# Part of a w2 block loaded ahead of wo in 125 and 3 rows, and three filler products on TensorE

## The chip, the cores and the metric

The kernel runs on one core of one Trainium2 chip. The metric is the device time of one execution in microseconds; lower is better. A core has the engines TensorE (PE in the profile, PEld for its loads of weights), VectorE (DVE), ScalarE (ACT), GpSimd (POOL) and SyncE (SP), and sixteen DMA engines that carry the loads which SP issues.

## The reference

A decode step for two sequences with one new token each. Attention of 32 query heads over 8 key and value heads in a window of the last 4096 positions, and beside it a dense layer with the Mish activation; a sigmoid gate mixes the two.

```
x: (2, 1, 512)   W = 4096, Dh = 128, F = 1792
q = (x @ wq) as (2, 32, 1, 128)
k, v = the last W positions of k_cache, v_cache, each of 8 heads used by 4 query heads
a = softmax(q k^T * Dh^-0.5) v, as (2, 1, 4096), @ wo          # wo: 4096 x 512
h = x @ w1 + b1;  b = (h * tanh(softplus(h))) @ w2             # w1: 512 x 1792, w2: 1792 x 512
g = sigmoid(sum(x * gate_w))
out = g * a + (1 - g) * b
```

All data are f32.

## The kernel before

Everything that is large is loaded once, by SP, into three buffers of 128 x 16384 f32 that are used in turn (`stream`): `wq`, then one tile for each of the eight key and value heads (`kv0` to `kv7`), then `w12`, then `wo`. Before the launch the arrays are laid out so that a load is 128 rows, one for each partition, each of them contiguous.

For each head, TensorE multiplies the queries with the keys (`scores`, L148), VectorE takes the maximum (L151), ScalarE the exponential (L153), TensorE turns the result (`turned`, L160) and multiplies it with the values (`values`, L172). The load of the next head into a buffer is issued when the products of the head that had the buffer are done. In all of these products the array is split into four strips of 32 columns, one product in each, so four run side by side. An f32 product appears as two passes in the profile.

The tile `w12` holds w1 (7168 columns), the first four heads' rows of wo (2048 columns) and w2. w2 has 14 blocks of 128 rows, 512 columns each; the first seven come with w1 in one load. The tile `wo` holds the other 28 heads' rows, in two loads, of 20 and of 8 heads (`WO`, L291). The other seven blocks of w2 come last, in three loads of 4, 2 and 1 blocks (`CUTS`, L294), into the rest of the tile `w12`. So SP's queue at the end is: kv7, w12, wo (20 heads), wo (8 heads), w2 (4 blocks), w2 (2), w2 (1). The tile `wo` needs the buffer of kv6, so SP waits for that head's products between the issue of w12 and that of wo.

What TensorE does at the end, in this order: `hidden` (x with w1), `outputs` (the normalized heads), then `project` (L305) with the four heads of wo that lie in `w12`, `middle` with the seven blocks of w2 that came with w1, the 28 heads in `wo`; all of these add into `acc`. Then `output(1)` (`finish`, L315) with the first four of the late blocks of w2, into `fin`; `finish(fold2, asum)`, which adds a copy of `acc` into `fin`; `output(2)` and `output(3)` with the last blocks. VectorE copies `fin` to `res` (L348) and SP stores it (L349). `pin` keeps the order of the products as written. Ahead of the store, SP waits until the last eight loads have landed (L343).

Of the kernel before, what the change touches and what calls it, by code (L numbers as in the profile page):

```python
# [8 lines left out]
F32 = mybir.dt.float32  # L9
# [4 lines left out]
P = 128  # L14
B = 2
D = 512
# [8 lines left out]
NJ = 4  # L25
# [6 lines left out]
FC = F // P  # L32
# [7 lines left out]
CUTS = (0, 7, 11, 13, 14)  # L40
WO = (1, 6, 8)
ROWS = (24, 104)
WIDE = 2 * Q - B
AHEAD = DC * F + WO[0] * REP * D


@with_exitstack
def decode_kernel(ctx: ExitStack, tc: tile.TileContext, res, stored, small, wqh, wqt, kv_in, w12, wo, w2, out):
    nc = tc.nc
# [5 lines left out]
    ps_s = ctx.enter_context(tc.tile_pool(name="ps_s", bufs=2, space=bass.MemoryType.PSUM))  # L55
    ps_1 = ctx.enter_context(tc.tile_pool(name="ps_1", bufs=1, space=bass.MemoryType.PSUM))

    loads = []

    def load(name, *parts):  # L60
        t = stream.tile([P, 2 * CHUNK], F32, tag="s", name=name)
        x = 0
        for cols, src in parts:
            loads.append(nc.sync.dma_start(t[:, x : x + cols], src))  # L64
            x += cols
        return t
# [20 lines left out]
    ones = const.tile([P, P], F32, name="ones")  # L87
# [54 lines left out]
    pin = tc.keep_in_program_order  # L142

    def scores(kv, t):
        sc = ps_s.tile([P, 512], F32, tag="sc", name=f"sc{kv}")
        for m in range(BN):
            for j in range(NJ):
                nc.tensor.matmul(sc[Q * j : Q * j + Q, :], qz[:, kv, m * Q : m * Q + Q],  # L148
                                 t[:, (m * NJ + j) * 512 : (m * NJ + j + 1) * 512],
                                 start=(m == 0), stop=(m == BN - 1))  # L150
        nc.vector.tensor_reduce(mx[:, kv : kv + 1], sc, axis=AX.X, op=ALU.max, negate=True)  # L151
        p = work.tile([P, 512], F32, tag="p", name=f"p{kv}")
        nc.scalar.activation(p, sc, AF.Exp, bias=mx[:, kv : kv + 1], accum_out=ls[:, kv : kv + 1])  # L153
        return p
# [11 lines left out]
    def values(kv, pT, t, c0=0, c1=NT):  # L166
        if kv % 2 == 0 and c0 == 0:
            pair[0] = ps_1.tile([P, 2, BN * DH], F32, tag="o", name=f"o{kv}")
        o = pair[0][:, kv % 2, :]
        for c in range(c0, c1):  # L170
            for j in range(NJ):
                pin(nc.tensor.matmul(o[Q * j : Q * j + Q], pT[:, c, Q * j : Q * j + Q],  # L172
                                     t[:, (c * NJ + j) * 512 : (c * NJ + j + 1) * 512],
                                     start=(c == 0), stop=(c == NT - 1)))
        if kv % 2 and c1 == NT:
            wide = [P, 2 * BN, DH]
            om = single.tile(wide, F32, tag="om", name=f"om{kv}")
            ov = om.rearrange("p (k m) d -> p k m d", m=BN)
            nc.vector.tensor_tensor(  # L179
                ov, pair[0].rearrange("p k (m d) -> p k m d", m=BN),  # L180
                pick[:, None, :, None].to_broadcast([P, 2, BN, DH]), op=ALU.mult)
            nc.vector.tensor_reduce(od[:, kv - 1 : kv + 1], ov.rearrange("p k m d -> p k d m"),  # L182
                                    axis=AX.X, op=ALU.add)
# [89 lines left out]
    for kv in range(HKV):  # L273
        t = load(f"kv{kv}", (2 * CHUNK, kv_in[kv]))
        p = scores(kv, t[:, :CHUNK])
# [7 lines left out]
            r = shares(kl)  # L283
        values(kv, pT, t[:, CHUNK:], 2, NT)
    w12_t = load("w12", (AHEAD + CUTS[1] * D, w12))

    def flat(src, cuts, size):
        for f0, f1 in zip(cuts, cuts[1:]):
            yield (f1 - f0) * size, src[f0 * size * P : f1 * size * P].rearrange("(p x) -> p x", p=P)

    wo_t = load("wo", *flat(wo, [f - WO[0] for f in WO], REP * D))  # L291
    x = AHEAD + CUTS[1] * D
    for cols, src in flat(w2, [f - CUTS[1] for f in CUTS[1:]], D):
        loads.append(nc.sync.dma_start(w12_t[:, x : x + cols], src))  # L294
        x += cols
    hidden(w12_t)
# [6 lines left out]
    def project(j, lhsT, rhs, n):  # L303
        n_col[j] += 1
        return nc.tensor.matmul(acc[Q * j : Q * j + Q, :], lhsT, rhs,  # L305
                                start=(n_col[j] == 1), stop=(n_col[j] == n))
# [5 lines left out]
    def finish(lhsT, rhs):  # L312
        for j in range(NJ):
            y = j % 2 * (Q - B)
            nc.tensor.matmul(fin[Q * j : Q * j + Q, :], lhsT[:, y : y + Q], rhs[:, j * P : (j + 1) * P],  # L315
                             start=(done[0] == 0), stop=(done[0] == n_fin - 1))
        done[0] += 1

    def middle(f0, f1):
        for f in range(f0, f1):  # L320
            x = AHEAD + f * D
            pin(project(f % NJ, actT[:, f, :], w12_t[:, x : x + D], n_of[f % NJ]))

    first = WO[0] * REP
    for x in range(HQ):
        w = w12_t[:, DC * F + x * D :] if x < first else wo_t[:, (x - first) * D :]
        if x == first:
            middle(0, CUTS[1])
        pin(project(x % REP, oT[:, x, :], w[:, :D], n_of[x % REP]))
    asum = work.tile([P, D], F32, tag="p", name="asum")  # L330
    nc.scalar.copy(asum, acc)

    def output(i):
        for f in range(CUTS[i], CUTS[i + 1]):
            x = AHEAD + f * D
            finish(act2[:, f - CUTS[1], :], w12_t[:, x : x + D])
# [72 lines left out]
```

## Time and profile before

| | |
|---|---|
| median of three runs | 219.33 us (219.32 to 219.41) |
| profiled execution, span from the first to the last instruction | 217.6 us |
| TensorE busy | 113.0 us (52%) |
| DMA, rate over the span | 419 GB/s |
| chain that ended last | DMA 77%, PE 18% |
| mean granted TensorE clock | 0.867 |

For the profiled execution the profile gives the span and no other time; 1.7 us of the median lie around it. In the profile, a line such as `206.00 7.91 PE acc L305 x56` of a chain or a timeline gives the start and the length in us, the engine, the tile written, the line of the kernel and the number of instructions. In a table of windows each row gives a stretch, its length, the busy time and number of instructions of PE, PEld, DVE, ACT and POOL, then the clock granted to TensorE (1.00 is full speed), the share of the sixteen DMA engines at work, and GB/s. The queue q1 carries the loads and the store, q8 the engines' own instructions.

### The profile page before, as it was taken

The page shows a single profiled execution, that of the slowest core. Times are in us where ns is not written, and L with a number is a line of the kernel's source. Part 1 is how long each engine was busy: PE and PEld are TensorE (multiplying, and loading weights), DVE is VectorE, ACT ScalarE, POOL GpSimd, SP SyncE. Part 2 cuts the span into 40 slices and gives each one's busy share as a digit, 9 for nine tenths or more (in the row PEclk, how much of TensorE's full clock was granted, in tenths as well). Part 3 has the DMA queues.
Part 4 walks back from the last instruction along what each step waited for, and adds up shares of the span by engine and source line. Part 5 has one row for each costly group of instructions (what it writes and reads, how often), then busy time and mean ns, then how long its engine had stood idle before and what let it go on. Part 6 is the DMA issues. An engine that isn't in the chain of part 4 may idle for free.

```text
span 217.6 us, 1836 instructions
## 1 busy us (share of the span) xinstructions
PE 113.0 (52%) x822; PEld 33.8 (16%) x822; DVE 21.5 (10%) x32; ACT 15.5 (7%) x34; POOL 8.0 (4%) x30
## 2 busy tenths in 40 slices
PE   0000798477046608543660754286075418758596
PEld 0000322112011102101110210012011001214123
DVE  0000000010001230100123010010501001251000
ACT  2000001111001100200110020002002000301001
POOL 8000000000000000000000000000000000102100
PEclk9999999979658985995998599769759967999979
DMA  9797988898899889989998999899989999989892
GB/s 361 337 506 337 581 385 385 385 569 385 385 398 566 385 376 446 518 385 398 446 497 385 410 434 506 385 422 422 497 385 434 410 432 452 452 364 482 375 404 113
DMA packets 2550, 91.38 MB, mean 420 GB/s; under 512 B 416, under 2 KB 496, under 8 KB 752
## 3 DMA queue, kind: packets, MB, share of 16 engines
q1 hardware_dynamic: 2544, 91.28, 97.3%
q8 instruction: 6, 0.10, 0.2%
HBM read 91.24 MB, written 0.04 MB: 419 GB/s over the span
## 4 chain that ended last, share of the span: by engine, by line
DMA 77%; PE 18%; ACT 2%; DVE 1%; SPq 1%; issue 0%; ACTq 0%
DMA kv<-in_kv 61%; DMA wo<-in_wo 16%; PE sc L148 7%; PE o L172 5%; PE acc L305 4%; ACT p L153 1%; DVE mx L151 1%; PE pp L160 1%; PE fin L315 1%; ACT pT L161 1%; SPq L64 0%; SPq L70 0%; DVE res L348 0%; ACTq L161 0%; ACTq L153 0%
## 5 line engine op out<-in xcount | busy, mean ns | idle before, releaser
L148 PE MATMUL sc<-kv,qz 128*32 128x512 f32 x256 | 44.1, 851 | 54.1 <-DMA kv<-in_kv 54.1
L172 PE MATMUL o<-kv,pT 128*32 128x512 f32 x256 | 29.5, 596 | 5.8 <-ACT pT L161 5.8
L128 PE MATMUL qp<-wq,x 128*32 128x512 f32 x64 | 12.1, 799 | 23.0 <-POOL x L92 23.0
L148 PEld LDWEIGHTS sc<-kv,qz 128*32 128x32 f32 x256 | 9.9, 150 | 87.6 <-DMA kv<-in_kv 60.7
L151 DVE TENSOR_REDUCE mx<-sc 128x1 f32<-128x512 f32 x8 | 5.5, 691 | 112.4 <-PE sc L148 112.4
L153 ACT ACTIVATE p<-sc,mx 128x512 f32<-128x512 f32 x8 | 5.5, 687 | 131.2 <-DVE mx L151 131.2
L160 PE MATMUL pp<-ident,p 128*128 128x128 f32 x32 | 5.3, 287 | 12.1 <-ACT p L153 12.1
L172 PEld LDWEIGHTS o<-kv,pT 128*32 128x32 f32 x256 | 7.3, 109 | 20.9 <-issue 13.1
L305 PE MATMUL acc<-wo,padded 128*32 128x512 f32 x56 | 7.9, 728 | 2.2 <-DMA wo<-in_wo 2.2
L182 DVE TENSOR_REDUCE od<-om 128x256 f32<-128x1024 f32 x4 | 7.6, 1900 | 0.1
L128 PEld LDWEIGHTS qp<-wq,x 128*32 128x32 f32 x64 | 2.5, 137 | 28.9 <-POOL x L92 23.0
L179 DVE TENSOR_TENSOR om<-o,pick 128x1024 f32<-128x1024 f32 x4 | 4.9, 1225 | 19.3 <-PE o L172 19.3
L196 POOL TENSOR_TENSOR ms<-ms,top 8x64 f32<-8x64 f32 x2 | 0.6, 309 | 159.0 <-DVE top L194 159.0
L160 PEld LDWEIGHTS pp<-ident,p 128*128 128x128 f32 x32 | 3.4, 140 | 18.6 <-ACT p L153 18.6
L161 ACT COPY pT<-pp 128x512 f32<-128x512 f32 x8 | 4.7, 585 | 6.2 <-PE pp L160 6.2
L235 PE MATMUL hp<-w,x 128*32 128x512 f32 (+1 forms) x32 | 3.6, 543 | 2.3 <-DMA w<-in_w 2.3
L305 PEld LDWEIGHTS acc<-wo,padded 128*32 128x32 f32 x56 | 2.1, 129 | 8.0 <-issue 4.9
L305 PE MATMUL acc<-w,padded 128*32 128x512 f32 x22 | 2.8, 601 | 0.4 <-DVE padded L226 0.4
L117 DVE RECIPROCAL g<-g 128x2 f32<-128x2 f32 x1 | 0.2, 166 | 22.4 <-POOL g L116 22.4
L134 PE MATMUL qt<-ident,qs 128*128 128x128 f32 x8 | 1.3, 287 | 1.4 <-ACT qs L131 1.4
L112 PEld LDWEIGHTS zp<-xg,ones 128*128 128x128 f32 x8 | 1.8, 327 | 1.7 <-issue 1.7
L131 ACT ACTIVATE qs<-qp 128x512 f32<-128x512 f32 x2 | 1.2, 597 | 10.6 <-PE qp L128 10.6
(65 smaller groups left out, 31.3 us busy)
## 6 DMA issues: line engine op xcount, KB each, us to landing
wq<-in_wqt SPq DMA_DIRECT2D x1, 7168.0 KB, 21.4
w<-in_w SPq DMA_DIRECT2D x1, 6400.0 KB, 41.1
wo<-in_wo SPq DMA_DIRECT2D x1, 5120.0 KB, 34.8
wo<-in_wo SPq DMA_DIRECT2D x1, 2048.0 KB, 39.3
wq<-in_wqh SPq DMA_DIRECT2D x1, 1024.0 KB, 4.9
w<-in_w SPq DMA_DIRECT2D x1, 1024.0 KB, 41.3
w<-in_w SPq DMA_DIRECT2D x1, 512.0 KB, 42.0
w<-in_w SPq DMA_DIRECT2D x1, 256.0 KB, 42.1
```

The source lines that it names most:

```text
L128: nc.tensor.matmul(qp[Q * k : Q * k + Q, :], x32[:, c, :], w[:, c, k, :], start=(c == 0), stop=(c == DC - 1))
L148: nc.tensor.matmul(sc[Q * j : Q * j + Q, :], qz[:, kv, m * Q : m * Q + Q], t[:, (m * NJ + j) * 512 : (m * NJ + j + 1) * 512], start=(m == ...
L151: nc.vector.tensor_reduce(mx[:, kv : kv + 1], sc, axis=AX.X, op=ALU.max, negate=True)
L153: nc.scalar.activation(p, sc, AF.Exp, bias=mx[:, kv : kv + 1], accum_out=ls[:, kv : kv + 1])
L160: pin(nc.tensor.transpose(pp[:, c, :], p[:, c * P : (c + 1) * P], ident))
L161: nc.scalar.copy(pT, pp)
L172: pin(nc.tensor.matmul(o[Q * j : Q * j + Q], pT[:, c, Q * j : Q * j + Q], t[:, (c * NJ + j) * 512 : (c * NJ + j + 1) * 512], start=(c == 0 ...
L179: nc.vector.tensor_tensor(ov, pair[0].rearrange("p k (m d) -> p k m d", m=BN), pick[:, None, :, None].to_broadcast([P, 2, BN, DH]), op=ALU ...
L182: nc.vector.tensor_reduce(od[:, kv - 1 : kv + 1], ov.rearrange("p k m d -> p k d m"), axis=AX.X, op=ALU.add)
L235: nc.tensor.matmul(hp[Q * j : Q * j + Q, :n], x32[:, c, :], w[:, c, j * FG * P : j * FG * P + n], start=(c == 0), stop=(c == DC - 1))
L305: return nc.tensor.matmul(acc[Q * j : Q * j + Q, :], lhsT, rhs, start=(n_col[j] == 1), stop=(n_col[j] == n))
L315: nc.tensor.matmul(fin[Q * j : Q * j + Q, :], lhsT[:, y : y + Q], rhs[:, j * P : (j + 1) * P], start=(done[0] == 0), stop=(done[0] == n_fi ...
```

## The change

Of the first late block of w2, 384 of its 512 columns (`LOW`) are taken out of the load of four blocks and are loaded right behind w12, ahead of wo, by two loads: partitions 0 to 124 (`MOST` = 125 rows) and partitions 125 to 127 (3 rows), of 1536 bytes a row. The load of four blocks shrinks from 2048 to 1664 columns; the host lays w2 out accordingly. The tile, its columns and what is computed from them stay the same. On TensorE, three products of the constant `ones` (128 x 128) with the first 3 x 512 columns of w1 stand between `middle` and the first product with the tile `wo`; they write the tile `idle` in PSUM, which nothing reads.

```diff
+MOST = 125
+LOW = (NJ - 1) * P
...
     w12_t = load("w12", (AHEAD + CUTS[1] * D, w12))
+    at = AHEAD + CUTS[1] * D
+    for p0, p1 in ((0, MOST), (MOST, P)):
+        loads.append(nc.sync.dma_start(
+            w12_t[p0:p1, at : at + LOW], w2[p0 * LOW : p1 * LOW].rearrange("(p x) -> p x", p=p1 - p0)))
...
     wo_t = load("wo", *flat(wo, [f - WO[0] for f in WO], REP * D))
-    x = AHEAD + CUTS[1] * D
-    for cols, src in flat(w2, [f - CUTS[1] for f in CUTS[1:]], D):
+    x = at + LOW
+    ends = [0] + [(f - CUTS[1]) * D - LOW for f in CUTS[2:]]
+    for cols, src in flat(w2[P * LOW :], ends, 1):
         loads.append(nc.sync.dma_start(w12_t[:, x : x + cols], src))
         x += cols
...
         if x == first:
             middle(0, CUTS[1])
+            idle = ps_s.tile([P, 512], F32, tag="sc", name="idle")
+            for k in range(3):
+                pin(nc.tensor.matmul(idle, ones, w12_t[:, k * 512 : (k + 1) * 512], start=True, stop=True))
...
-    w2 = np.concatenate([w2[f:t].transpose(1, 0, 2).ravel() for f, t in zip(CUTS[1:], CUTS[2:])])
+    w2 = w2[CUTS[1] :].transpose(1, 0, 2).reshape(P, (FC - CUTS[1]) * D)
+    ends = [0, LOW] + [(f - CUTS[1]) * D for f in CUTS[2:]]
+    w2 = np.concatenate([w2[:, x0:x1].ravel() for x0, x1 in zip(ends, ends[1:])])
```

## The prediction

> **What bounds the kernel now.** I read the page first (span, engines, queues, chain), then the chain in order of time, then the timeline of the last 17 us.
>
> ```profile
> span 217.6 us, 1836 instructions
> PE 113.0 (52%) x822; PEld 33.8 (16%) x822; DVE 21.5 (10%) x32; ACT 15.5 (7%) x34; POOL 8.0 (4%) x30
> q1 hardware_dynamic: 2544, 91.28, 97.3%
> q8 instruction: 6, 0.10, 0.2%
> HBM read 91.24 MB, written 0.04 MB: 419 GB/s over the span
> DMA 77%; PE 18%; ACT 2%; DVE 1%; SPq 1%; issue 0%; ACTq 0%
> ```
>
> The loads fill 97.3% of the sixteen DMA engines' time. No byte is added or taken away by this change, so up to about 200 us nothing can move; all of it is decided in the tail, where the chain leaves the DMA engines and runs on TensorE:
>
> ```profile
> 171.11 34.85 DMA wo<-in_wo
> 205.96 0.04 issue
> 206.00 7.91 PE acc L305 x56
> 213.91 1.83 PE fin L315 x64
> 215.74 0.02 issue
> 215.77 0.29 DVE res L348
> ```
>
> The first wo load lands at 205.96, 56 passes of wo's products take 7.91 us, 64 passes of the last stage 1.83 us, then the copy and the store. But DMA is not far behind. The queue's issues and the time from issue to landing:
>
> ```profile
> 171.97 1.43 SPq L294 DMA_DIRECT2D w<-in_w  x3
> w<-in_w SPq DMA_DIRECT2D x1, 1024.0 KB, 41.3
> w<-in_w SPq DMA_DIRECT2D x1, 512.0 KB, 42.0
> w<-in_w SPq DMA_DIRECT2D x1, 256.0 KB, 42.1
> ```
>
> Three issues in 1.43 us start at about 171.97, 172.45 and 172.95, so w2's three blocks land at 213.3, 214.5 and 215.1. What must still follow the last landing is the last block's eight passes:
>
> ```profile
> 213.73 1.06 PE L315 MATMUL fin<-w,padded 128*32 128x128 f32 x32
> 214.62 0.42 PE L315 MATMUL fin<-asum,padded 128*32 128x128 f32 x8
> 214.86 0.84 PE L315 MATMUL fin<-w,padded 128*32 128x128 f32 x24
> ```
>
> Eight passes more cost 1.06 - 0.84 = 0.22 us, so the last eight of the 24 alone take 0.84 - 0.44 = 0.40 us. After the landing at 215.1 and 0.04 us of issue that is an end at 215.55 by DMA alone, against 215.74 by TensorE. **Two chains end within 0.2 us of each other**; whoever shortens only one gets 0.2 us at most.
>
> Both have a visible fault. TensorE's is the clock:
>
> ```profile
> 203.14:206.55 3.41, 1.23 (x14) 0.25 (x12) 0.00 (x0) 0.00 (x0) 0.00 (x0) 1.00 0.86 368
> 206.55:209.96 3.41, 3.41 (x24) 0.89 (x20) 0.00 (x0) 0.00 (x0) 0.00 (x0) 0.50 1.00 425
> 201.01 2.81 PE L305 MATMUL acc<-w,padded 128*32 128x512 f32 x22 [0.43 <-DVE padded L226]
> ```
>
> In the windows, the third number from the right is the granted clock. After a stretch with 1.23 us of work in 3.41 it was 0.50 for the next 3.41 us: while wo's first products ran. The DMA engines' fault is that they do not finish together:
>
> ```profile
> 212.80:213.00 0.20, 0.20 (x8) 0.13 (x4) 0.00 (x0) 0.00 (x0) 0.00 (x0) 1.00 0.99 389
> 213.20:213.40 0.20, 0.20 (x8) 0.02 (x1) 0.00 (x0) 0.00 (x0) 0.00 (x0) 1.00 0.49 195
> 213.60:213.80 0.20, 0.20 (x8) 0.07 (x4) 0.00 (x0) 0.00 (x0) 0.00 (x0) 1.00 0.40 164
> 214.00:214.10 0.10, 0.10 (x16) 0.10 (x8) 0.00 (x0) 0.10 (x1) 0.00 (x0) 1.00 0.33 123
> 214.40:214.60 0.20, 0.20 (x16) 0.12 (x6) 0.00 (x0) 0.17 (x1) 0.00 (x0) 1.00 0.26 102
> 214.70:214.80 0.10, 0.10 (x12) 0.10 (x12) 0.00 (x0) 0.00 (x0) 0.00 (x0) 1.00 0.01 0
> ```
>
> The last two numbers are the share of the sixteen engines at work and GB/s. Until 213.0 all work; by 213.6 six are left (0.40 x 16), by 214.4 four, and at 214.7 none. Ten are done at 213.0 to 213.5, six run about 1.3 us longer. Six is also the number of packets on the instruction queue above. I read it so: each fetch of instructions went in between the loads of another engine and set it back by 1.3 us (none is set back twice: the tail would be 2.6 us long).
>
> **The change part by part.** *Removed from the tail:* w2's first block loses 384 columns, 128 x 1536 bytes, on each engine eight rows of 1536 bytes = 12,288 bytes. At full share the window above moved 425 GB/s, 26.6 per engine: 0.46 us less behind wo, on all sixteen.
>
> *Added ahead of wo:* the same 196,608 bytes as loads of 125 and 3 rows. Every load of the trace has 128 rows (the store 80), so how 125 are shared no row shows. I take equal shares: 125 = 5 x 25, five engines get 25 rows each, 38,400 bytes; of the other three rows one each goes to three of these. The nearest price for rows this short is the 2 KB rows of the last block, 102 GB/s at a share of 0.26: 24.5 GB/s per engine, 1.57 us; by the 26.6 of long rows it is 1.44. I take 1.55. The five engines are then 1.55 us later at wo, and 1.55 - 0.46 = 1.1 us later at the end. The bounds from both sides: shared evenly over sixteen, 0.46 us each, nothing at the end; all on one engine, 7.4 us.
>
> [...]
>
> *SP's queue* gets two more issues, at 0.33 to 0.48 us each. They stand behind w12's issue, where SP then waits for wo's buffer until 171.11, so they delay nothing:
>
> ```profile
> 152.92 0.33 SPq L64 DMA_DIRECT2D w<-in_w  x1
> 171.11 0.82 SPq L64 DMA_DIRECT2D wo<-in_wo  x2
> SPq L343 <- DMA w<-in_w: 4.2, 3, 2.4
> SPq L349 <- DVE res L348: 0.9, 1, 0.9
> ```
>
> The wait ahead of the store (L343) covers the last eight loads as before, and SP then still waited 0.9 us for the copy; it binds at no point.
>
> *Three products of the constant with w1:* each is a matmul over the whole array and 512 columns, two passes as every f32 product here. Four passes of 32 columns that run side by side come every 0.43 us, from the values' products:
>
> ```profile
> 50.37 3.69 PE o L172 x32
> ```
>
> (32 passes in 3.69 us less the 0.6 us of the last one give about 0.43 per four.) A pass over all columns takes as long as the four: 6 x 0.43 = 2.6 us. They start when the last pass of w2's first products has streamed, about 203.7, and end at 206.2 to 206.4. The stretch from 203.14 to 206.55 is then filled, so I expect the clock to stay at 1.00. Who waits behind them on TensorE are wo's products; wo's load lands at 205.96 on the late engines, and on five clean ones at 205.96 - 1.3 + 1.55 = 206.2. So they cost 0 to 0.4 us in their place, and 56 passes then take 13 x 0.43 + 0.6 = 6.2 us instead of 7.91: done at 212.6 instead of 213.9. They write a PSUM buffer whose last reader, head 7's exponential, was done long before.
>
> *The sum, if the five engines are clean ones.* Late engines: last data at 214.7 - 0.46 = 214.25. The five: 213.0 to 213.5 plus 1.1 = 214.1 to 214.6. Last data therefore between 214.25 and 214.6, and the landing, 0.4 us behind the data as now (214.7 to 215.1), at 214.65 to 215.0; I take 214.8. TensorE by then: first block of w2 at 213.3 - 0.46 = 212.85, or 213.0 on the five; 1.06 us of passes to 214.1, the sum's eight passes inside that wait, second block at 214.05 to 214.2. TensorE waits for the last block, so DMA sets the end: 214.8 + 0.04 + 0.40 = 215.24 instead of 215.74, **0.50 us less**. Copy and store are unchanged. The profiled span is 217.6 and the median 219.33, so 1.7 us lie around the span; I leave them as they are: 219.33 - 0.50 = **218.83 us**, with 218.65 to 219.0 by the bounds.
>
> **The rivals.** *A late engine among the five (slower).* No view numbers the engines. If one of the six that a fetch set back also takes 25 rows, it ends 1.1 us after 214.7: landing at 216.2, end at 216.64, 0.9 us more, 220.2. If it is one of the two that were done by 214.2, landing 215.7, 0.45 us more, 219.8. It decides as soon as a single late engine is among the five, because an engine may take 0.46 us over its present load and no more. [...]
>
> *The 128 rows are shared evenly after all.* Then it is only a reordering; the last landing stays at 215.1 and the end at 215.55: 219.14.
>
> *The half-speed stretch is not in the timed executions.* It hangs on where a 3.41 us stretch falls on the wait of 2.2 us before wo. If the timed runs had none, they ended by DMA at 215.55 already, and clean engines give 0.31 us less: 219.02. [...]
>
> *The clock drops nevertheless, or the three products take longer:* wo's products from 206.3 at 7.91 us, then 1.83: end at 216.05, 0.3 us more, 219.64.
>
> *All 125 rows on one engine:* 7.4 - 0.46 - 1.3 us after the present last data: about 225.
>
> **How the numbers follow.** Clean engines 0.60 (of it 0.10 with no slow stretch before), a late one among the five 0.25, even shares 0.08, clock or products 0.05, one engine 0.02. A measurement of this kernel tells about 0.2%, 0.44 us, from no change. Faster by more than that is most of the clean case with the slow stretch: 0.44. Within 0.2%: the rest of the clean case, even shares, and a little of the others: 0.29. Slower: 0.27. The likeliest case alone spans 218.65 to 219.0; the range is 218.6 to 219.9, which takes in even shares, the clock, and the milder half of the late engine, and leaves out 220.2 and 225.
>
> **What would show it.** Right: granted clock 1.00 from 206.5 to 210; some 6.2 us for wo's 56 passes; a share of the DMA engines that falls to zero within about 0.4 us in place of 1.7; the chain's last DMA step is w, not wo, and ends at 214.8. Wrong: a share of 0.06 to 0.3 that lasts past 214.7 (a late engine got more), or an unchanged staircase (even shares); a clock of 0.50 after 206.5; a seventh packet on the instruction queue, 1.3 us more on one engine.

## The result and the profile after

The changed kernel takes 220.60 us in the median against 219.32; the ratio is 1.0055, with an interval of 1.0039 to 1.0071. It is slower by half a per cent, and it scatters: eleven runs lie between 219.49 and 223.91 us, where those of the kernel before lie between 219.15 and 220.06. The profiled execution is the slowest of them, 223.91 us; the ratios here and below leave out executions over 1.5% above the fastest of their kernel (here 223.91 and 223.54), so a reading of this profile counts only where the profile of another kernel below shows the same.

The page of the changed kernel, against 217.6 us and 113.0 us of TensorE before:

```profile
span 222.0 us, 1850 instructions
PE 123.4 (56%) x828; PEld 38.0 (17%) x828; DVE 21.4 (10%) x32; ACT 15.5 (7%) x34; POOL 8.0 (4%) x30
q8 instruction: 6, 0.10, 0.2%
DMA 59%; PE 24%; another core or an unknown queue 10%; ACT 3%; DVE 2%; issue 1%; SPq 1%; POOL 0%; ACTq 0%; DVEq 0%; POOLq 0%
```

Six passes were added, yet TensorE is busy 10 us longer. The end of its chain of waits (start, length, what):

```profile
203.66 5.34 PE acc L312 x22
209.00 2.98 PE idle L338 x6
...
212.33 5.92 PE acc L312 x53
...
219.04 1.12 PE fin L322 x32
220.19 0.29 DVE res L358
```

The last wait for a DMA is gone from the tail. From w12's landing on TensorE waits for no DMA and is late: the 22 first products with wo and w2 take 5.34 us (before: 2.81), the fillers follow on the path, and wo's products begin at 212. wo's first load had landed at 206.8, 32.8 us after its issue at 174.01:

```profile
174.01 0.84 SPq L66 DMA_DIRECT2D wo<-in_wo  x2
```

```profile
wo<-in_wo SPq DMA_DIRECT2D x1, 5120.0 KB, 32.8
```

Why it is late, its timeline and its table of windows say (clock, share of the DMA engines and GB/s are the last three numbers):

```profile
194.77 5.33 PE L237 MATMUL hp<-w,x 128*32 128x512 f32 x32 [3.29 <-DMA w<-in_w]
```

```profile
195.72:199.14 3.42, 3.42 (x23) 0.88 (x19) 0.00 (x0) 0.00 (x0) 0.00 (x0) 0.50 1.05 455
...
202.55:205.96 3.41, 2.98 (x16) 1.18 (x19) 0.46 (x2) 0.00 (x0) 1.16 (x5) 0.50 0.91 394
205.96:209.38 3.42, 3.42 (x15) 0.84 (x8) 0.00 (x0) 0.00 (x0) 0.00 (x0) 0.50 1.02 438
```

The half clock, which stood under wo's products before, now stands under x with w1 and under the first products, ahead of the fillers. The DMA side, from the same view:

```profile
186.00:204.00 18.00, 13.05 (x94) 5.30 (x96) 5.07 (x10) 1.76 (x5) 2.33 (x9) 0.86 1.00 411
```

```profile
214.00:214.20 0.20, 0.20 (x8) 0.08 (x1) 0.00 (x0) 0.00 (x0) 0.00 (x0) 1.00 0.67 266
...
214.40:214.60 0.20, 0.20 (x8) 0.07 (x4) 0.00 (x0) 0.00 (x0) 0.00 (x0) 1.00 0.61 236
...
214.80:215.00 0.20, 0.20 (x8) 0.07 (x4) 0.00 (x0) 0.00 (x0) 0.00 (x0) 1.00 0.32 123
215.00:215.20 0.20, 0.20 (x8) 0.13 (x4) 0.00 (x0) 0.00 (x0) 0.00 (x0) 1.00 0.01 0
```

The bytes moved as planned: from 214.0 to 214.6 nine to eleven of the sixteen engines work (0.58 to 0.67), not six. The trace has every packet with its start, its length and its bytes. If each is joined to the one that starts where it ends, five engines carry nearly all rows of 1536 bytes, and none of the five is one of the six late engines (ends at 214.6 to 214.7, and at 215.0 to 215.1): five and six make the eleven. But the end is 215.0 and not 214.25 to 214.6; it was 214.7 before. The engines to which nothing was added are done by 213.3 to 213.8, where before they were done at 213.0 to 213.5, although each had 0.46 us less to carry.

Two suspects remain: the fillers, and the loads.

### The profile page after: what moved, and what is told of

The parts are those of the page before. It is cut to its first block, busy times and chain, and to the rows that moved or that the text cites. A ratio compares the mean times of both kernels' runs of the same rounds, so it can differ in the third digit from the quotient of the medians.

```text
span 222.0 us, 1850 instructions
## 1 busy us (share of the span) xinstructions
PE 123.4 (56%) x828; PEld 38.0 (17%) x828; DVE 21.4 (10%) x32; ACT 15.5 (7%) x34; POOL 8.0 (4%) x30
## 4 chain that ended last, share of the span: by engine, by line
DMA 59%; PE 24%; another core or an unknown queue 10%; ACT 3%; DVE 2%; issue 1%; SPq 1%; POOL 0%; ACTq 0%; DVEq 0%; POOLq 0%
DMA kv<-in_kv 59%; PE sc L150 10%; PE acc L312 5%; PE o L174 5%; ACT p L155 1%; PE idle L338 1%; DVE mx L153 1%; PE fin L322 1%; PE pp L162 1%; PE ol L226 1%; ACT pT L163 1%; SPq L66 0%; PE ht L252 0%; POOL ms L198 0%
## 5 line engine op out<-in xcount | busy, mean ns | idle before, releaser
L150 PE MATMUL sc<-kv,qz 128*32 128x512 f32 x256 | 45.9, 882 | 49.3 <-DMA kv<-in_kv 49.3
L174 PE MATMUL o<-kv,pT 128*32 128x512 f32 x256 | 32.5, 647 | 5.8 <-ACT pT L163 5.8
L237 PE MATMUL hp<-w,x 128*32 128x512 f32 (+1 forms) x32 | 5.3, 749 | 3.3 <-DMA w<-in_w 3.3
L312 PE MATMUL acc<-wo,padded 128*32 128x512 f32 x56 | 6.4, 593 | 0.0
L312 PE MATMUL acc<-w,padded 128*32 128x512 f32 x22 | 5.3, 1061 | 0.4 <-DVE padded L228 0.4
L312 PEld LDWEIGHTS acc<-wo,padded 128*32 128x32 f32 x56 | 3.1, 110 | 2.4
L338 PE MATMUL idle<-w,ones 128*128 128x512 f32 x6 | 3.0, 644 | 0.0
L237 PEld LDWEIGHTS hp<-w,x 128*32 128x32 f32 x32 | 1.4, 137 | 7.2 <-DMA w<-in_w 4.2
L322 PE MATMUL fin<-w,padded 128*32 128x128 f32 x56 | 2.3, 274 | 0.0
## 6 DMA issues: line engine op xcount, KB each, us to landing
wo<-in_wo SPq DMA_DIRECT2D x1, 5120.0 KB, 32.8
```

Source lines behind the costliest of these rows:

```text
L237: nc.tensor.matmul(hp[Q * j : Q * j + Q, :n], x32[:, c, :], w[:, c, j * FG * P : j * FG * P + n], start=(c == 0), stop=(c == DC - 1))
L338: pin(nc.tensor.matmul(idle, ones, w12_t[:, k * 512 : (k + 1) * 512], start=True, stop=True))
```

## The experiments

Theory A: the fillers use up the time in which TensorE waited for wo, so that half clock ahead of them reaches the end. Theory B: the loads cause the loss, by a later w12 and wo. Later, theory C: the loads cost by the way their rows are dealt to the engines.

**The loads without the fillers** (changed kernel):

```diff
-            idle = ps_s.tile([P, 512], F32, tag="sc", name="idle")
-            for k in range(3):
-                pin(nc.tensor.matmul(idle, ones, w12_t[:, k * 512 : (k + 1) * 512], start=True, stop=True))
```

> The loads of 125 and 3 rows without the three filler products. Theory A (the fillers use up the time in which TensorE used to wait for wo, so that a stretch at half clock ahead of them now reaches the end; the loads cost little): 219.4 to 219.7 us, with a spread under 0.5 us, since the last landing of the changed kernel, 215.4, and 0.44 us after it end 0.1 to 0.2 us later than before. Theory B (the loads cause it: they stretch the other engines' packets, w12 lands 0.7 us later, and TensorE's chain starts later): 220.4 to 220.6 us with the spread of the changed kernel.

Measured: 220.08 us (219.48 to 221.03), ratio 1.0028 [1.0016, 1.0041]. This is between the two expectations, so the loads carry a part of the loss. The chain of this kernel:

```profile
170.92 35.66 DMA wo<-in_wo
...
206.62 7.78 PE acc L312 x56
214.40 1.84 PE fin L322 x58
```

wo lands 0.62 us later than before (206.58 for 205.96), and the products behind it run at half clock as they did before (7.78 and 7.91 us). Its windows:

```profile
206.41:209.82 3.41, 3.20 (x16) 0.80 (x20) 0.00 (x0) 0.00 (x0) 0.00 (x0) 0.50 1.02 437
```

```profile
186.00:204.00 18.00, 13.48 (x116) 5.29 (x117) 5.22 (x11) 1.76 (x5) 2.85 (x11) 1.00 0.99 411
```

From 186 to 204 us the engines were as busy as before (0.99) but moved 411 GB/s and not 426: the kernel before has this row:

```profile
186.00:204.00 18.00, 13.81 (x113) 5.34 (x113) 5.42 (x11) 1.76 (x5) 2.85 (x11) 1.00 0.99 426
```

15 GB/s over 18 us are 0.27 MB, 0.63 us of the whole rate. The transfers take longer; nobody waits. The packets say which ones. The rows of 1536 bytes are under way from 191.6 to 193.9 us, mostly five at a time. wo's first load has 128 rows of 40,960 bytes: before, one took 2.00 us, from 192.95 on, right behind an instruction packet (192.02, 0.94 us), and all others 1.51; here 22 take 1.63 to 2.28 us, and all 22 start between 191.5 and 194.1.

**The fillers without the loads** (kernel before, with the three lines above added):

> The three filler products without the new loads. Theory A: median 219.8 to 220.5 us, spread over 1 us, the slow executions with half clock in the stretch of x with w1 or of the first products with wo and w2. Theory B: 219.0 to 219.3 us, at most 0.2 us faster than before, since w12 lands when it did before.

Measured: 219.56 us (219.17 to 221.62), ratio 1.0014 [0.9993, 1.0036]: the scatter of theory A, but a median between the two expected ranges and a shift that is not clear of none. The profiled execution, 219.94 us, is one of the upper half; its chain:

```profile
200.96 4.47 PE acc L305 x22
205.43 2.77 PE idle L331 x6
208.20 6.15 PE acc L305 x56
214.35 1.83 PE fin L315 x64
```

The first products run at half clock (granted 0.50 from 201.8 to 205.2 us; 4.47 us for 2.81), so the fillers end at 208.2 instead of 206.4, 2.3 us behind wo's landing at 205.9 in this execution. In exchange wo's products take 6.15 us, as forecast.

**One load of 128 rows at the same place, no fillers** (the kernel of the loads alone):

```diff
-    for p0, p1 in ((0, MOST), (MOST, P)):
+    for p0, p1 in ((0, P),):
```

> The same 384 columns at the same place in one load of 128 rows, no fillers. If the loads cost by their shape (rows on five engines that cross the other engines' transfers): w12 lands 41.1 us after its issue as before, not 42.1, and the time is 219.2 to 219.4 us. If they cost by their place ahead of wo: as the loads of 125 and 3 rows, w12 at 42 us.

Measured: 219.52 us, ratio 1.0007 [0.9998, 1.0016]. Its windows:

```profile
186.00:204.00 18.00, 13.97 (x108) 5.61 (x110) 5.46 (x11) 2.46 (x8) 2.85 (x11) 0.92 1.00 428
```

The same bytes stand at the same place, and the rate stays at 428 GB/s; each of the 128 rows of wo's first load takes 1.51 us. So the shape costs, not the place. The time is a little above the expected range, and w12 landed 42.3 us after its issue, the sign that was named for the other case. But the issue came 1 us earlier than before (151.90 for 152.92), and the landing is at 194.2 for 194.0: here the time from the issue is no measure of the loads.

**Fillers ahead of x with w1 too** (the kernel with the fillers alone):

```diff
+    early = ps_s.tile([P, 512], F32, tag="sc", name="early")
+    for k in range(3):
+        pin(nc.tensor.matmul(early, ones, t[:, k * 512 : (k + 1) * 512], start=True, stop=True))
     hidden(w12_t)
```

> Three filler products with the last head's tile ahead of x with w1, and the three ahead of wo's products; no new loads. Theory A: the clock is full from the last head on, the fillers ahead of wo end by 206.4, and DMA sets the end: 219.0 to 219.3 us with a spread under 0.5 us. If it is the fillers' own 2.6 us that cost, and not the clock ahead of them: 220 us or more, slower than with the second three alone.

Measured: 219.48 us, ratio 1.0005 [0.9993, 1.0017], but from 219.11 to 223.83. The median is nearer theory A's range than the rival's, but the narrow spread is missing: seven of ten runs lie below 219.7, the others at 220.33, 222.51 and 223.83. So more fillers do not make the clock safe. The profiled execution, 219.46 us, has no half clock in the tail; what the runs at 220.33 and above have, no profile shows.

**112 and 16 rows** (the loads alone):

```diff
-MOST = 125
+MOST = 112
```

> [...] Theory C (what costs is that engines write to partitions that another engine is writing): between 219.7 and 220.1 us, as the loads of 125 and 3 rows; w12 lands later than 41.3 us after its issue. Theory D (what costs is that five engines carry it all): 219.4 to 219.6 us, as the load of 128 rows.

Measured: 219.98 us (219.96 to 220.62, four runs), ratio 1.0040 [1.0025, 1.0055], as 125 and 3 rows. In the packets these rows are not confined to five engines (up to twelve at a time), so it is not that five carry them. The table of windows does not show the loss, as it counts a packet's bytes where the packet starts:

```profile
186.00:204.00 18.00, 13.36 (x117) 5.26 (x115) 5.01 (x10) 1.76 (x5) 2.84 (x11) 1.00 1.02 425
```

With each packet's bytes spread over the time it took, the rate from 186 to 204 us is 417 GB/s here, 416 with 125 and 3 rows, 432 with one load of 128 rows and 433 before; 25 of the 128 rows of wo's first load take 1.58 to 2.04 us. In the profiled execution the loss is DMA's; its chain waits for w2's first late block until 213.86, for 213.3 before:

```profile
175.02 38.84 DMA w<-in_w
213.86 0.04 issue
213.90 2.31 PE fin L322 x58
```

**The loads of 125 and 3 rows behind wo** (the loads alone, the loop moved):

```diff
     wo_t = load("wo", *flat(wo, [f - WO[0] for f in WO], REP * D))
+    for p0, p1 in ((0, MOST), (MOST, P)):
...
     x = at + LOW
```

> The loads of 125 and 3 rows moved behind wo's two loads, ahead of the rest of w2; no fillers. Theory C: w12 and wo land as before (206.0), TensorE's chain is as before, and the stretch of the other engines' packets falls on w2's last loads: 219.3 to 219.8 us. If the engines' balance is what counts and the cost is a later w12 and wo alone: 219.1 to 219.3 us, at most a little faster than before.

Measured: 219.65 us, ratio 1.0017 [1.0007, 1.0026], inside theory C's range. With w12 and wo's first load landing as before (194.0 and 205.9) the loads still gain nothing; they lose 0.3 us. In the profiled execution TensorE waits 1.10 us for wo's second load, which lands at 211.5, so there its chain runs through this load, and not through the last loads of w2 as expected.

**128 rows and the three fillers** (changed kernel, with the edit of one load):

> One load of 128 rows ahead of wo, and the three fillers. If the changed kernel's 1.2 us are the sum of the shape of the loads (0.4 to 0.6) and of fillers behind a w12 and a wo that land later (0.6): 219.8 to 220.2 us. If the fillers cost only together with loads of 125 rows: 219.5 us, as the load of 128 rows alone.

Measured: 219.99 us (219.27 to 223.28), ratio 1.0039 [1.0017, 1.0061]: the fillers cost 0.47 us on top of 219.52 (0.58, if each median is taken against the runs of the kernel before beside it, 219.31 and 219.42). This pair shows them alone, for both profiled executions have half clock from 201.1 or 201.2 on. Timelines, with the fillers and (second) without:

```profile
200.71 4.47 PE L312 MATMUL acc<-w,padded 128*32 128x512 f32 x22 [0.43 <-DVE padded L228]
205.11 2.84 PE L338 MATMUL idle<-w,ones 128*128 128x512 f32 x6
...
208.12 6.18 PE L312 MATMUL acc<-wo,padded 128*32 128x512 f32 x55
```

```profile
201.20 4.41 PE L312 MATMUL acc<-w,padded 128*32 128x512 f32 x22 [0.43 <-DVE padded L228]
...
206.65 4.50 PE L312 MATMUL acc<-wo,padded 128*32 128x512 f32 x40 [0.83 <-DMA wo<-in_wo]
```

Without them TensorE had caught up and waited 0.83 us for wo; the slack took the half clock. With them wo's products begin some 1.5 us later. The windows of half clock, with the fillers and without:

```profile
201.23:204.64 3.41, 3.41 (x22) 0.77 (x14) 0.00 (x0) 0.00 (x0) 0.41 (x3) 0.50 1.10 473
```

```profile
201.12:204.53 3.41, 3.33 (x16) 0.75 (x19) 0.29 (x2) 0.00 (x0) 0.64 (x3) 0.50 1.10 476
```

**Twice the columns** (the loads alone):

```diff
-LOW = (NJ - 1) * P
+LOW = 2 * (NJ - 1) * P
```

> 768 columns in place of 384 by loads of 125 and 3 rows ahead of wo, no fillers. If the cost is the loads' (a later wo, by shape or by bytes): twice the 0.66 us of the loads alone, 220.6 to 221.0 us, and wo's first load lands near 207.8 us, the five engines' 3.1 us more being the last. If it was chance of the clock: 219.8 to 220.2 us.

Measured: 222.15 us (221.46 to 223.51, four runs), ratio 1.0139 [1.0099, 1.0179]. This is more than twice the loss; in the profiled execution, the slowest of the four, wo lands at 209.06 and not at 207.8. Chain and window:

```profile
171.57 37.49 DMA wo<-in_wo
209.06 0.04 issue
209.10 8.88 PE acc L312 x56
```

```profile
186.00:204.00 18.00, 13.46 (x115) 5.59 (x118) 5.39 (x11) 2.23 (x8) 2.84 (x11) 1.00 1.01 391
```

391 GB/s at nearly the same share: 35 GB/s lost, over twice the 15.

**Two loads of 128 rows and 192 columns** (the loads alone):

```diff
-    for p0, p1 in ((0, MOST), (MOST, P)):
+    for x0, x1 in ((0, LOW // 2), (LOW // 2, LOW)):
         loads.append(nc.sync.dma_start(
-            w12_t[p0:p1, at : at + LOW], w2[p0 * LOW : p1 * LOW].rearrange("(p x) -> p x", p=p1 - p0)))
+            w12_t[:, at + x0 : at + x1], w2[P * x0 : P * x1].rearrange("(p x) -> p x", p=P)))
...
-    ends = [0, LOW] + [(f - CUTS[1]) * D for f in CUTS[2:]]
+    ends = [0, LOW // 2, LOW] + [(f - CUTS[1]) * D for f in CUTS[2:]]
```

> [...] Theory C (crossing costs): 219.4 to 219.6 us, as one load of 128 rows, and wo's first load lands by 206.7. If two loads or short rows cost in themselves: 219.9 to 220.1 us.

Measured: 219.41 us, ratio 1.0008 [0.9999, 1.0018], and 428 GB/s:

```profile
186.00:204.00 18.00, 13.52 (x95) 5.10 (x99) 4.91 (x9) 1.76 (x5) 2.84 (x11) 0.85 1.00 428
```

Neither two loads nor rows of half the length cost, and again each row of wo's first load takes 1.51 us. What the two slow shapes have in common, and the two others not, is a row count that is not 128.

**One filler, and six, without the loads** (the kernel with the fillers alone):

```diff
-            for k in range(3):
+            for k in range(1):     # and, in the second kernel, range(6)
```

> One filler product in place of three, no new loads. It ends by 204.6 at full clock and by 207.1 where the products ahead of it run at half clock. Theory A (fillers cost where they end behind wo's landing): 219.2 to 219.4 us, with less spread than with three, at most 0.15 us faster than before, since DMA then sets the end at 215.55.

> Six filler products in place of three, no new loads. Theory A: they end at 208.8 at the earliest, 2.8 us behind wo's landing; then 6.2 and 1.83 us: an end at 216.9 or later, 220.4 us as the lowest, and 222 and more where half clock comes ahead. If DMA set the end with fillers too: 219.2 to 219.6 us as the lower half of the runs with three.

Measured: one filler 219.32 us (219.14 to 219.68), ratio 0.9997 [0.9987, 1.0006]; six 222.33 us (220.72 to 223.82, four runs), ratio 1.0135 [1.0090, 1.0179]. Both are as theory A says. The chain with six, in an execution without any half clock in the tail:

```profile
203.61 5.35 PE idle L331 x12
208.96 6.15 PE acc L305 x56
215.11 1.83 PE fin L315 x64
```

**The changed kernel with one filler:**

```diff
-            for k in range(3):
+            for k in range(1):
```

> The changed kernel with one filler in place of three. Theory A with C (the loads cost 0.6 us by crossing, the fillers cost where they end behind wo): 219.9 to 220.2 us, as the loads alone, and no run above 221.2. If fillers and these loads disturb each other in another way (a later w12 that sends the clock down): 220.4 us or more, as the changed kernel.

Measured: 219.53 us (219.40 to 219.88), ratio 1.0008 [0.9998, 1.0017]. This is better than either expectation: not only is the fillers' loss gone, most of the loads' loss too. Its timeline and its chain:

```profile
204.16 1.13 PE L338 MATMUL idle<-w,ones 128*128 128x512 f32 x2
...
206.56 4.50 PE L312 MATMUL acc<-wo,padded 128*32 128x512 f32 x40 [0.92 <-DMA wo<-in_wo]
```

```profile
175.00 38.34 DMA w<-in_w
213.34 0.04 issue
213.38 2.33 PE fin L322 x58
```

In this execution TensorE keeps the clock, and the filler still ends 0.9 us ahead of wo's products. So most of the 0.66 us of the loads alone was a later wo with half clock behind it; where TensorE keeps the clock, DMA sets the end, and what these loads cost there, 0.13 us between the medians, is not clear of none. That it is the filler that keeps the clock is likely, not shown: both kernels with one filler spread over 0.5 us only, the loads alone over 1.55, but the profile of 112 and 16 rows has full clock behind wo's landing too, with no filler and 1.45 us of work in the 3.41 us ahead.

No kernel here beats the one before by more than can be measured; one filler without the loads comes nearest.

## Why the prediction was wrong

**The gain of 0.46 us at the tail: right as bytes, lost as time.** The step that failed is the price of the added loads: 1.55 us on the five engines and nothing on the others, with the late engines at 214.7 - 0.46. Five engines with 25 rows each were the author's estimate, shown by no run before the change; the changed kernel's packets put nearly all rows on five. That the engines' present load was unequal, and that the five are not late ones, the same packets show (eleven engines until 214.6). But the others did not keep their pace: 411 GB/s for 426 at the same share, with rows of wo that took up to 2.24 us for 1.51; and the new rows took each of the five about 2.1 us (10.5 us of packets in all), not 1.55. The last data came at 215.0, not 214.25 to 214.6. The price belonged on every engine: 0.63 us of the whole rate, more than the 0.46 taken away. The sign that the share would fall to zero within 0.4 us did not follow from the prediction's own sum, which left the other five engines without anything added; measured, the share falls from 213.6 to 215.0.

The bytes were costed by engine alone. The runs say that the row count of a load counts as well: 128 rows, 428 GB/s and no clear loss (ratios 1.0007 and 1.0008); 125 and 3 or 112 and 16 rows, a loss of 0.3 to 0.4%, on five engines or on up to twelve at a time. Why, is not shown: theory C's times came in (219.98, 219.65 and 219.41 us), but which engine wrote which partition none of the views shows, and no run separates the writing of a row from its reading. What is shown is the dependence on the row count, and that the other loads' rows take longer while such rows are under way (up to 2.28 us for 1.51).

**wo's first load at 206.2: 206.6 to 206.8**, by the same error. Of the other rivals, a late engine among the five, even shares over all sixteen, and all rows on one engine are ruled out by the packets: five engines carry them, and eleven work until 214.6.

**"They cost 0 to 0.4 us in their place": the second step that failed.** Between the medians, leaving the fillers out gives back 0.52 us of the 1.28, leaving the loads out 1.04, and keeping one filler of three 1.07; the two losses are not a simple sum. The step took the clock ahead of the fillers as 1.00, where the profile before showed 1.00. The prediction's own third rival had the slow stretch missing in the timed executions, and priced only its absence behind wo (a gain of 0.31 us in place of 0.50), not its presence ahead of the fillers. In the profiles half clock began at 206.55 before, at 206.41 with the loads alone, at 201.12 with 128 rows and at 202.55 after, for 3.41 us in the first three and for 6.83 us in the last, and the starts do not lie whole multiples of 3.41 us apart (0.14, 5.43 and 4.00 us from the first). The wait of 2.2 us for wo was not idle capacity, but what takes up a half clock ahead (1.6 us in the kernel with 128 rows, where 0.83 us of the wait were left); that the kernel before stays within 1 us over all its runs fits this. Three fillers take that away: 0.47 to 0.58 us on top of the load of 128 rows, and single runs of 221 to 224.

The rival "the clock drops nevertheless, or the three products take longer" (219.64, chance 0.05) had the right engine at the end, but put the half clock under wo's products and not ahead of the fillers, and had too small a size and chance.

**Right:** two chains within 0.2 us of each other, as the kernel with one filler and no loads shows: it keeps the clock and its last product ends, by DMA, at 215.57 for 215.74; 6.2 us for wo's products at full clock (5.92 for 53 passes, 6.15 to 6.18 elsewhere); 0.43 us for a pass over all columns (twelve of them, with six fillers, took 5.35 us, six took 2.77); no seventh instruction packet; SP's queue. There SP did wait once more, for head 7's load, and it cost nothing, since w2's loads had 30 us of others before them:

```profile
SPq L301 <- DMA kv<-in_kv: 2.9, 1, 2.9
```

**Open:** how often half clock falls where. Each kernel was profiled in one execution, and the loads alone (TensorE late) and 112 rows (DMA late) show different ends. Why loads of 125 and 3 or of 112 and 16 rows slow the rows beside them is open too.

## What to carry to other kernels

Here a wait on the critical engine was spare time that took up a stretch at half clock (1.6 us of it in the kernel with 128 rows); fill such a wait sparingly (beside these loads one product of 1.1 us took 0.55 us off the median, three of 2.8 us added 0.52), and check the sum with the half clock placed ahead of the filler, not only where this profile has it. To use DMA engines that finish early, do not expect a load with another row count to run beside the others for nothing (125 and 3 rows cost 0.66 us between the medians here): see whether the rows of the loads around it take longer while it is under way. GB/s over a window is a coarser sign (with 112 and 16 rows it fell by 1, by the packets' own times by 16). Where two chains end together, cost each edit on both.

## What the runs showed of the hardware

- Loads of 125 and 3 rows, or of 112 and 16, of 1536 bytes between loads of 128 rows slowed the load beside them: 22 to 25 of 128 rows of 40,960 bytes took 1.58 to 2.28 us for 1.51. Over 18 us that is 416 and 417 GB/s for 433 by the packets' own times, and 389 with rows twice as long; loads of 128 rows of 1536 or 768 bytes did not (432 and 431, no slower row).
- One product of 1.13 us in the wait ahead of wo was followed by full clock in both profiled executions that had it (2.25 and 2.91 us of work in the 3.41 us ahead); a stretch with 1.23 us of work (the kernel before) or 1.38 (the loads alone) was followed by half clock, one with 1.45 (112 and 16 rows) by full clock.
- Where half clock fell on them, the same 22 passes took 4.41 to 5.34 us, for 2.81.
